# Five tiles of the last layer share their first and last score columns in 32x64 array tiles, under a new written-out order

## The chip, the cores and the metric

The kernel runs on one core of one Trainium2 chip. Its engines work side by side, each through its own list of instructions in order: TensorE (PE for matmuls, PEld for their weight loads), VectorE (DVE), ScalarE (ACT), GpSimd (POOL), and SyncE (SP), which here only issues DMAs. They wait for each other by semaphores. The metric is the time of one execution on the device in microseconds; less is better.

## The reference

A sequence of 2048 tokens of 512 features goes through four residual layers, x = x + f(layernorm(x)): linear attention (A), sliding-window attention (B), and both once more with the same weights. Each has 32 heads of 16 features.

```python
def _A_ref(x, wqkv, wo):
    phi = lambda t: jnp.where(t > 0, t + 1, jnp.exp(t)) + 1e-6
    pq, pk = phi(q), phi(k)
    kv = jnp.einsum("bhsd,bhse->bhde", pk, v)
    ...
    o = num / den
def _B_ref(x, wqkv, wo):
    scores = jnp.einsum("bhqd,bhkd->bhqk", q, k) * (Dh ** -0.5)
    mask = (idx[:, None] - idx[None, :] >= 0) & (idx[:, None] - idx[None, :] < W)   # W = 256
    p = _softmax(jnp.where(mask, scores, -1e9), axis=-1)
    o = jnp.einsum("bhqk,bhkd->bhqd", p, v)
```

In B a query sees itself and the 255 tokens before it. All values are bf16 in memory; matmuls accumulate in f32.

## The kernel before, in words

**Tiles.** The 2048 tokens are 16 tiles of 128, called j = 0 to 15 here. "Tiles ten to fourteen" of the change are j = 9 to 13. Activations stay in the core's memory from the first layer to the last.

**Scores of a sliding-window layer** (`b_scores`, `b_far`). Scores are computed with keys on the partitions. A tile's keys are two blocks (b = 0, 1) of 64; the 128 partitions of a block are 64 keys times two heads. The 32 heads are 16 pairs: four groups (f) of four (gq). A key of block b is seen by the queries from 64b of its tile on, over 64 + 255 places: a window of 320 columns. The first 64 are partly masked (a key does not see earlier queries), the last 64 as well (a query 256 later does not see it), the 192 between are whole. The window is computed in two pieces:

- `b_scores`, four times a tile (block b, groups f and f+1): 8 matmuls (L634) of 256 columns from column 0 of the window on. A matmul uses a 32-row by 128-column part of the array, and gq = 0 to 3 run in four such parts at once, into four banks of PSUM. Then two ACTIVATEs (L644) of 128x1024 take the exponential of two banks each into the buffer `P`, and a mask on DVE (L652) clears the forbidden part of the first 64 columns.
- `b_far`, once for each tile that has a tile two places later: 32 matmuls (L723) of the last 64 columns, for all f, b and gq, two ACTIVATEs (L732) of 128x1024, and two masks ("mf"), each on DVE (L704) or POOL (L703).

`P` has four slots in the last layer, used by j modulo 4. `b_values` (L753) multiplies the exponentials with the values; tile j's products read the slots of tiles j, j-1 and j-2, and of the far columns only those of tile j-2. Then come a reciprocal, a division, a transpose by DMA, the output projection and the residual.

**Beside it.** For later tiles the layer before's output (L400), the layer norm (statistics L361 and L362 on DVE, two small steps L363 and L364 on POOL, normalisation L365 on DVE, transposes by DMA) and the projections to queries, keys (L414) and values (L400) run ahead. Their results are evicted from PSUM by ACT or DVE, as the table says.

**What sets the order.** `Plan` adds all operations of the program to a list with what they read and write. `place` decodes `TABLE`, a long literal that holds three things: the order of all operations, the engine of each (where there is a choice), and the PSUM bank of each result. `synchronise` turns dependences into semaphore waits. `play` then emits each engine's operations in that order. So the order isn't computed at build time: it was made elsewhere, by a planner that replays the program, which the file does not contain. Each engine works strictly in the order written; an operation that waits holds all that stands behind it on its engine.

`PACK` says for which layer and tiles the window is computed in another way (`b_edge`); in the kernel before it is empty, so this function, though written, is not used.

Of the kernel before, what the change touches and what calls it, by code (L numbers as in the profile page):

```python
# [217 lines left out]
PACK = {}  # L218
# [5 lines left out]
def bass_view(x, free):  # L224

    return bass.AP(x.tensor, x.offset, [x.ap[0]] + free)


class Plan:
# [583 lines left out]
    def middle(self, ph):  # L813
# [67 lines left out]
    r"c-qx@1GF_svTkM|BlEXy+qP}nwr$(CZQHhO+vck}r|*5!Z@Oo?d-~nAZk@e%)sBq#BI5g^a@AfZlu{~$0;LryR$&yWuqvD~D!huXLaGNYf=Zwws)XvEi=-aA",  # L881
    r"L@KgMtdgiqN>mh;RNZ$?)pPgAJ#m@UXq8N5QOQ*^)k9@fR;5+VRSK0&jZy1WcGW_~QaRLEHCM$}#Z^@G%=J_oR7zD-#Zlu_OVvw_SFKbu_0&yJ2UTlTOZ8Tz",
    r")I1ekwNY(VP}N7(RvT4k^<AY?snjM_M0HW~Rb16hHBfa_Jk?O8R|`~86<haJ`PD?#PqkN*R8F-}HBxm|f0aiKP(M@#)j|DKG1Nd+Or=(v)nrvq9a0(97FA7k",
    r"RF_p(6;mBngH#%|NKH|LReg0tby8Q<QFT=fRa4b5wN-Uf*VH!kRFzSSRd=;rEm1?%b+uIOP&bs)&(sXHQ$1HRRcN(Ll~p12G?iB!S6ZJ?%N6JsDwmqBLg_gA",
    r"q*|$7s?a*Wo~3T8S1PT(rNZdAdWFiZPN~}}oerXQtJ5mI-lf87)baEk6;9t(XH*7Fy0I#tU#pC|pk_T=WzuKW9Cc3_{YJ&tqKByjx`2AChN~v3rY@-7sS)bF",
    r"s-;J&@cO+fq$B9kYLxn@N~nlBvo5TQ=t%m5imbEfggUEsDv{2ntxl}7>nJ*jE~=C2LaLZ{y0}iJE2|PZs!py;>Iy1{4z5b+e5$rCtb(bEx{l7N>*?XTk}j>A",
    r">&m){uA)|{7P_jgrbp=Nx`uA4SF5_Zl4_;bsHVD|ZmgT>J*u2)qZ{fby1s6$%d5Srfj+0!sz$o4KCddOeQKm$r$*`h>VlfBtE<s^j=rc4=`p&b`lPC=HF~U`",
    r"s}JjO`m>s+$Lj}bf_|tDsEK;MKBC*}NqT`^t1qdAdYWFOzo_YYonEXTsmZ#7e&c57y?TmXuV?Cxx|9B@rs`RGgWjh*>y7%d-mkmp<$9BTtXAmFdWn9bw&<05",
    r"ss5&}=w-UA4gy#8QGG)Pg=_kj?xu^uDt$~BhhT71AJ+%;6CFgK&`<SAy;YZhQ+k_zrh~%{9aJCG+x2t3Q<sEb`nrChcj?tSD!kOuAOr;0r644n)*<vOeMX0Z",
    r"(hwT%=;&}(hk<jthPtQE>xb@wzN@?IG7t}X=!^OkB!JVfN0)`_@LI=*a&QJ>K@GUAW5WoD2{mCP#DV*|HY9_D@J7GYF(5fS(C_p^Jqj-A6gmZ@)Q|LT9T&>O",  # L890
    r"d!0%@)~TQZeATISY8VY+Asmc>G>}G*g$NKHB0@zN2X$aPoP|U%0qQ~}hy;nD9-M=ox)!v6^N<88LsDo37hon_gjtXhT0&a*rY}Ji_^xL|1NfoSK_f^HKlN>B",
    r"2(96R&HxJP!ySkW8b0ZaFcI!Tc9;YJA9Wj;440uDTmgi}Ku|`1(QTouz6zNj3Y62Ibq>e^)gUJ{fvS)TGDB0C2hAWG<c2A*0H#8D&5#G?Lj|1|3^a#mS|A@R",
    r"ghh}QrolB>4A&t)SSSGPA-cW+OP~Wd=m;_NQdk9@Af{dhYhVt<(#v5kbcWT?ORs>Quo8Ofb+7^Y>4H!Q`s(!%2K(r+xE2b-6W9o^-7_cxn;;x+hNAEk!s7?1",
    r"h#%oORKhK=6?(xZsEoVe0Yt#wPz4`CM9ii8z<tQABjF?H3teCu&VZ_zM@Pon*bg2<6zm3Zu|MS1(=ng!3IiY>R>OgC2WQ|Qh>z9r4b;Fr&>h~wUbqK$u?O_m",
    r"@1Q2`gKaQCZ-*B!9bUp`*a5fTJ?w{McoV)r3OoR>;42)2*RTtc<4jD1QE{M7g5Mw-?u73!7@{L$VjKeLa3~ytx|k5tV+<Syvv4@X#MzhuQ(`8ZgGsR-X2w)l",
    r"A5&u%jD^kdFtos|SPPFpMy!o#uqCF&)>sD#+aO~ryocGaEgJj**)a~z#h=g!6JQQ(j5$%EU}roEO|T0tN5E!y47#Gm6__8pqs8OU4qv#H*dBZ0JiL!5paVX@",
    r"lh6YluEE&Y5er}t?1byEAojwC_|gT%ZnzeM;Rbw!y|EB(#6Gwln_^*n<u>7C%!Ng;FD}BO*bj5#V%&@ku^7(B;+O}Q;0`Q-3vd^{!G-u1^WjcxfP-{!9IS_6",
    r"UVMikaF~AULgF4AqE}-A+KZvEBo5W3a36-ogw!8P<4|0R1F#GZ!$h<SpWr|&i_7pSCZ;3!47cELJc?U!HzuJGcnp)$S8Ph#a6cxa@7Rn+Vsd(p%_#*9#&7rn",
    r"4`2&=iKFl%wxl0;5I^H~9F41J5FWx$xS9^*7(~iQt!OMVWun%UlG+f_8v1~#C=GqV%ybeB39Y5nbR5%?rJwj7(~+WA=;#EtrEH|>6awX-(>M;Z(-|C(K`0kZ",
    r"z_S>Xa??Z%M(1!6p2s|tlZsJRx`4syJ%ymxSb{##I?78OX+2%U;`EU&VIkT;ou~-qqmq<`I#YfsOyQ_E6`*!hkor(jYEPx8FLj{)^odH-0P07Vu?!8QD_E93",  # L900
    r"Q%KrKS1|((qVN=oBG5IgOxLj+g{JNlk#^H2ibOqVG=-%-G?pUMWK2(cX$nT6F;tGCQWg3_(WnAdrRWrfwox^jirc9?^`zmngTB&W>PjQ2It`&NG>%5lX8J}$",
    r"={p^u8dQmD(iS>I!zc!ArCt=1YSBSDLbYiW)u9`Blq%9q98b6K7)_v9bb%()aWZ_7CXw(A(tL?51IMN_beZbXSvpMh2zei!pmP+5_R~qKPv<EppQ0-ij89Vo",
    r"x=IZxIEQ4%*JvhPr%)V%XVG2yL9;0|N8}*<ljcw)&cbs^aaNv3k$E!Br$)4s7SI%GOxbuB-J>Qnl@`){ipmctE=A*M6pvc)LyFEf=n=K#=|p^s9@8U^Pt1?`",
    r"Cbi-xbeI=W7=FS}DK5w0BOH&P@@)#sQ8+#?rlTB=pYamP%i%dD=jRB#lw$ER%Evi5JKv$@l#8EHY+gYH_!zIG+<b;}@L4X(=lDDq=Qw<U^Kc?A#uvFHALr6s",
    r"kWX+SPROOWBbVUkT$np?8GgY<I01L&ww##TaS|@eNx40j<7E7j`*Jx<&i%Oyr{MC~fnRYyenTnwEmgn)+>^`mJL<~4xB_?M*W8<{@pDSWv$;FJpt;<GQ}Y}?",
    r"$$j`GRpeJRkSlQ;eoce8HCN_SJeaHV5I)UScqmWj8a$If@(ixYZ@3mO=TE$XXYop2%(b~HzvZP|hcog#Uc#C9GuP#1JdEFQJs!@hxIWM4%shfu^BNw>3wRW-",
    r"<u5#%)9^Z8$Z2^IkKs$4j>qzPZp!0$1E=T9{FSe82ENL5%|_nD+HB@)Jf62On5}%B(QM-zJb|}!Gv2`y`6kyhJGlYx;)dLur*I>l%8hw9Phv8AxC!6l_k5f8",
    r"@&~@d)A#`I<H>xG@A7^=#P|3<vw6S|`5R|8nap?2V}5WBlh@=jIZZZWOm6d&vzUBFnd~ON$!f$DFhPwq1x<b9OaoKcbTkc3CllT@GQmt|Gs^@wvrS`D$TTq#",
    r"OcyiQG&Ms^GZVx#H=#@m)76A9q0La!&9pILOi0t+v^70U5!24hF+I&x6VVJa?M+M5%M3RiOe+(~6g4AEKhxTbH2qCvQ_M^=1I#E>+=MmL&1f^wlrp`|7}LiL",
    r"G9}DdGsBcLea$!%&dfA>%y@Ijls0=!D4A<6n|)@3xne@gMl;V$FkxiAnP{$>O=f{PU<%1XbI?pOi%emuV^*6Ya>%?eQ_MB9##}eA%wx0G+%QkfOLNm~F;C4c",  # L910
    r"v)F7iVP%PlVxF0BveaxfQB8PxZVsDeCV~`|XlA`RVV0X>a>}eT5v91qG||mu6T`$ZCrt^tZ6e7EbH~Is+szwu*OZi%CXR_M`^{T(&#W?=O<Z%|yfbm+fhl9+",
    r"$`|v{lr=}pS98?FmmOxOIc6eDJUMQ@nfK<0DJ8E>6xn5dn$sq+*=?dq5_8rl`CvYpq((~ud1OABXp+n%lFuf(BsY~Mp_DT*#7Gsf^4-LgbEc}CH?c${iCi!s",
# [181 lines left out]
```

## Time and profile before

| | |
|---|---|
| runs shown | 416.35, 417.3, 420.33 us (median 417.3) |
| the profiled execution | 415.97 us |
| its span in the trace | 414.2 us, 17130 instructions |
| granted TensorE clock | 0.999 |
| busy, share of the span | PE 94%, DVE 84%, ACT 83%, PEld 62%, POOL 28% |
| ACTIVATEs for scores (L644, L732) | 256 and 56 |
| far masks on POOL, on DVE | 29, 27 |

The page counts busy time over the whole span. The layers differ in what limits them, so the stretches are what to look at: the second layer's scores run from about 60 us to 230 us, the last layer's from about 260 us to 406 us. A busy PE includes matmuls that are under way at the same time. "Wait" rows name the instruction that waited, what released it, the total, the number of times and the longest.

### The profile page before, as it was taken

The page shows a single profiled execution, that of the slowest core. Times are in us where ns is not written, and L with a number is a line of the kernel's source. Part 1 is how long each engine was busy: PE and PEld are TensorE (multiplying, and loading weights), DVE is VectorE, ACT ScalarE, POOL GpSimd, SP SyncE. Part 2 cuts the span into 40 slices and gives each one's busy share as a digit, 9 for nine tenths or more (in the row PEclk, how much of TensorE's full clock was granted, in tenths as well). Part 3 has the DMA queues.
Part 4 walks back from the last instruction along what each step waited for, and adds up shares of the span by engine and source line. Part 5 has one row for each costly group of instructions (what it writes and reads, how often), then busy time and mean ns, then how long its engine had stood idle before and what let it go on. Part 6 is the DMA issues. An engine that isn't in the chain of part 4 may idle for free.

```text
span 414.2 us, 17130 instructions
## 1 busy us (share of the span) xinstructions
PE 387.9 (94%) x7481; PEld 258.5 (62%) x7555; DVE 346.8 (84%) x803; ACT 345.8 (83%) x432; POOL 117.7 (28%) x211
## 2 busy tenths in 40 slices
PE   7999999999999999999999999999999989988886
PEld 3545676766575577565666777586757745556554
DVE  5997898989989988778978689989799687776575
ACT  2624449998999999999997245999999999999992
POOL 4784833111241243230112302220132215230111
PEclk9999999999999999999999999999999999999999
DMA  7545316632233624444213100353306623273361
GB/s 246 177 79 148 104 40 119 131 92 68 64 96 78 110 73 113 80 107 106 56 29 69 26 2 27 93 148 79 81 7 134 137 56 95 60 159 96 93 121 54
DMA packets 67555, 37.83 MB, mean 91 GB/s; under 512 B 48248, under 2 KB 62584, under 8 KB 67480
## 3 DMA queue, kind: packets, MB, share of 16 engines
q1 hardware_dynamic: 67040, 35.54, 36.7%
q8 instruction: 60, 0.98, 1.0%
q0 software_dynamic: 432, 1.18, 0.9%
q14 instruction: 15, 0.12, 0.1%
q10 hardware_dynamic: 8, 0.00, 0.0%
HBM read 6.29 MB, written 2.10 MB: 20 GB/s over the span
## 4 chain that ended last, share of the span: by engine, by line
PE 48%; ACT 35%; DVE 9%; DMA 5%; issue 2%; SPq 1%
ACT pb L644 22%; PE ps L400 17%; PE ps L414 13%; PE ps L753 7%; ACT pb L732 6%; ACT vp L644 5%; PE ps L634 5%; PE ps L475 2%; DMA XQ<-xn 2%; DVE stats L361 2%; DMA xres<-in_A_x_dram 2%; DVE xres L568 1%; DVE XQ L557 1%; PE ps L723 1%; ACT vp L732 1%
## 5 line engine op out<-in xcount | busy, mean ns | idle before, releaser
L644 ACT ACTIVATE pb<-ps 128x1024 bf16<-128x1024 f32 (+2 forms) x224 | 206.7, 1042 | 4.5 <-PE ps L634 3.7
L753 PEld LDWEIGHTS ps<-vB,pb 128*128 128x128 bf16 x2560 | 77.5, 96 | 11.7 <-issue 4.6
L753 PE MATMUL ps<-vB,pb 128*128 128x34 bf16 x2560 | 83.2, 177 | 1.1 <-ACT pb L644 0.6
L414 PE MATMUL ps<-xT,wBp 128*128 128x128 bf16 x1024 | 69.2, 219 | 1.2 <-DVE vp L586 0.5
L414 PEld LDWEIGHTS ps<-xT,wBp 128*128 128x128 bf16 x1024 | 59.2, 98 | 13.6 <-issue 4.4
L423 ACT ACTIVATE tE<-ps 128x512 bf16<-128x512 f32 x64 | 38.5, 612 | 34.3 <-PE ps L400 15.5
L363 POOL TENSOR_SCALAR ve<-mv 128x1 f32<-128x1 f32 x64 | 16.7, 261 | 172.6 <-DVE mv L362 170.5
L634 PE MATMUL ps<-XQ,kB 32*128 32x256 bf16 (+2 forms) x1024 | 49.6, 267 | 5.0 <-ACT vp L644 1.4
L732 ACT ACTIVATE pb<-ps 128x1024 bf16<-128x1024 f32 x50 | 49.6, 1066 | 0.4 <-PE ps L723 0.2
L568 DVE TENSOR_TENSOR xres<-ps,xres 128x512 bf16<-128x512 f32 x63 | 43.1, 685 | 7.6 <-PE ps L400 7.0
L400 PE MATMUL ps<-wA,XQ 128*128 128x512 bf16 x176 | 46.2, 379 | 2.7 <-issue 0.6
L652 DVE TENSOR_TENSOR pb<-pb,tri 128x512 bf16<-128x512 bf16 x112 | 44.7, 412 | 4.0 <-ACT pb L644 3.7
L703 POOL TENSOR_SCALAR_AFFINE_SELECT pb<-pb 128x1024 bf16<-128x1024 bf16 x26 | 29.8, 1148 | 62.9 <-DVE pb L652 32.6
L361 DVE BATCH_NORM_STATS2 stats<-xres 128x6 f32<-128x512 bf16 x64 | 43.6, 686 | 2.6 <-DMA xres<-in_A_x_dram 1.8
L364 POOL TENSOR_TENSOR rs<-ve,negh 128x1 f32<-128x1 f32 x64 | 37.8, 591 | 5.3
L634 PEld LDWEIGHTS ps<-XQ,kB 32*128 32x128 bf16 x1024 | 15.5, 92 | 33.6 <-ACT pb L644 9.2
L414 PE MATMUL ps<-XQ,wA 128*128 128x128 bf16 x512 | 34.7, 219 | 0.3 <-DVE o L766 0.3
L414 PEld LDWEIGHTS ps<-XQ,wA 128*128 128x128 bf16 x512 | 30.4, 98 | 5.7 <-DVE o L766 0.6
L400 PE MATMUL ps<-wBv,xT 128*128 128x512 bf16 x112 | 31.5, 380 | 2.2 <-issue 1.3
L400 PE MATMUL ps<-wBo,oT 128*128 128x512 bf16 x105 | 28.8, 380 | 4.2 <-issue 1.1
L400 PE MATMUL ps<-M,XQ 128*128 128x512 bf16 x112 | 30.7, 380 | 2.1 <-issue 1.0
L765 DVE RECIPROCAL rc<-ps 128x16 f32<-128x16 f32 x64 | 16.1, 252 | 19.3 <-PE ps L753 19.0
(110 smaller groups left out, 532.8 us busy)
## 6 DMA issues: line engine op xcount, KB each, us to landing
vB<-vS SPq DMA_DIRECT2D x64, 136.0 KB, 2.6
kB<-vp SPq DMA_DIRECT2D x64, 128.0 KB, 2.7
wA<-in_A_wqkv_dram SPq DMA_DIRECT2D x3, 512.0 KB, 4.6
out_dram<-xres POOLq DMA_DIRECT2D x9, 128.0 KB, 2.8
xres<-in_A_x_dram SPq DMA_DIRECT2D x2, 512.0 KB, 4.3
pb<-in_B_wqkv_dram SPq DMA_DIRECT2D x1, 1024.0 KB, 5.6
xres<-in_A_x_dram SPq DMA_DIRECT2D x3, 256.0 KB, 4.8
out_dram<-xres SPq DMA_DIRECT2D x6, 128.0 KB, 2.4
```

The lines of the kernel that those rows point to most:

```text
L361: self.on("DVE", "stats", lambda e: e.bn_stats(K.stats[:, t, :], K.xres[:, t, :]), key, dve(512), rd=[("xres", t)], wr=[("stats", t)])
L364: self.pow = self.on("POOL", "pow", lambda e: e.tensor_tensor(K.rs[:, t, :], K.ve[:, t, :], K.negh[:], ALU.pow), key + 0.03, (640, 690), r ...
L400: m = e.matmul(K.ps(ps), lhs(c), rhs(c), start=c == 0, stop=c == 3)
L414: m = e.matmul(K.ps(ps)[:, f * P:(f + 1) * P], w(c, f), xT(c), start=c == 0, stop=c == 3)
L423: self.on("ACT", "E", lambda e: e.activation(K.tE[:, s, :], K.ps(ps), ACT.Exp, bias=0.0), key, act(512), wr=[("tE", s)], ps=[ps])
L568: self.on("DVE", "res", lambda e: e.tensor_tensor(K.xres[:, t, :], K.ps(po), K.xres[:, t, :], ALU.add), key, dve(512), rd=[("xres", t)], w ...
L634: m = e.matmul(K.ps(ps[gq])[:, ns * i:ns * i + ns], K.kB[rows, j % 4, 2 * f + b, :, :], K.XQ[rows, f, q:q + ns], start=True, stop=True, ti ...
L644: return e.activation(out(2 * h, 2, ns), i, ACT.Exp, bias=0.0, scale=0.25)
L652: return e.tensor_tensor(x, x, K.tri[:, 0, sh:64].unsqueeze(1).unsqueeze(1).to_broadcast([P, 4, n, 64 - sh]), ALU.mult)
L703: return e.affine_select(out=x, in_=x, compare_op=ALU.is_ge, fill=0.0, base=-2, pattern=[[0, 16], [-2, 64]], channel_multiplier=1)
L732: return e.activation(far(h), i, ACT.Exp, bias=0.0, scale=0.25)
L753: m = e.matmul(K.ps(ps)[:, 34 * u:34 * u + 34], K.P((b // 2) % rp)[:, gq, f, o:o + P], K.vB[:, (b // 2) % 4, b % 2, r, :], start=i == 0, s ...
```

## The change

**The packing.** For the last layer, `PACK` now names j = 9 to 13. For these tiles `b_scores` computes the window's columns 32 to 287 instead of 0 to 255; it still has 8 matmuls of 256 columns and two ACTIVATEs of 128x1024, four times a tile. `b_edge` takes the place of `b_far` and computes what is left. Of the first 32 columns only the first 32 keys of a block are ever visible, and of the last 32 only the last 32 keys. So both halves share one bank row: the first 32 keys times the first 32 columns go to partitions 0 to 63, and the last 32 keys times the last 32 columns go to partitions 64 to 127. The old text of `b_edge` computed both for all keys and copied one half over ("gc"); the new one computes each with a 32-row by 64-column part of the array (eight at once), 64 matmuls of 32 columns. Two ACTIVATEs of 128x512 follow. They write the last 32 columns of the window; an operation on DVE ("ma", 64 partitions, 1024 elements each) copies partitions 0 to 63 from there to the first 32 columns and masks them. The diagonal mask ("md") then covers 32 columns where it covered 64. The two far masks stay as they are; they wait for the copy. The products of tile j wait for its copy too, since part of its first columns now comes from the edge.

**The table.** It is replaced as a whole. Read out, it holds 2553 operations where there were 2548 (the five copies). PE has 874 in both, DVE 802 in both, ACT 427 for 431, POOL 217 for 207, SP 233 for 234.

- ACT's order of the exponentials is nearly the old one; the far pairs of j = 9 to 13 are gone, and the edge pairs stand behind the first two to four exponentials of their own tile.
- Thirteen copies and evictions go from ACT to DVE, nine from DVE to ACT. Of those in the second layer's scores, three that ran on ACT between 147 and 157 us go to DVE.
- Of the far masks, seventeen go from DVE to POOL (eight of them in the second layer) and eight from POOL to DVE (three there).
- Four output DMAs go from POOL's queue to SP's, five the other way.
- On PE, DVE, POOL and SP many operations move by a place or two, some by more: the rearrangement of weights ("wp") and the setting of constants on POOL in the first 70 us, and the far masks.

```diff
-PACK = {}
+PACK = {3: (9, 10, 11, 12, 13, )}
...
             for f in range(4):
                 for b in range(2):
-                    q = P * j + 64 * b
                     for gq in range(4):
                         rows = slice(32 * gq, 32 * gq + 32)
-                        c = 128 * f + 64 * b
-                        m = e.matmul(K.ps(ps[gq])[:, c:c + 64], K.kB[rows, j % 4, 2 * f + b, :, :], bass_view(K.XQ[rows, f, q:q + 32], [[288, 2], [1, 32]]), start=True, stop=True, tile_position=(32 * gq, 0))
+                        c = 64 * f + 32 * b
+                        for u in range(2):
+                            q = P * j + 64 * b + 288 * u
+                            half = slice(64 * u, 64 * u + 64)
+                            m = e.matmul(K.PS[half, ps[gq].banks[0], c:c + 32], K.kB[rows, j % 4, 2 * f + b, 32 * u:32 * u + 32, :], K.XQ[rows, f, q:q + 32], start=True, stop=True, tile_position=(32 * gq, 64 * u))
...
-        self.pe("s", put, key, 1, 512, mode=(32, 128), occ=245, rd=[("kB", j % 4, 0), ("kB", j % 4, 1), ("XQ", j), ("XQ", j + 2)], ps=ps)
+        self.pe("s", put, key, 1, 256, mode=(32, 64), occ=540, rd=[("kB", j % 4, 0), ("kB", j % 4, 1), ("XQ", j), ("XQ", j + 2)], ps=ps)
...
-            side = lambda c, two=two: bass_view(K.PS[64:128, two[0].banks[0], c:c + 32], [[512 * (two[1].banks[0] - two[0].banks[0]), 2], [64, 8], [1, 32]])
-            self.on("DVE", "gc", lambda e, side=side: e.tensor_copy(side(0), side(32)), key, dve(512), ps=two)
...
-                return e.activation(edge(h), K.pair(two, [[128, 4], [64, 2], [1, 32]]), ACT.Exp, bias=0.0, scale=0.25)
+                return e.activation(edge(h), K.pair(two, [[64, 4], [32, 2], [1, 32]]), ACT.Exp, bias=0.0, scale=0.25)
...
 TABLE = (
-    r"c-qx@1GF_svTkM|BlEXy+qP}nwr$(CZQHhO+vck}r|*5!Z@Oo?d-~nAZk@e%)sBq#BI5g^a@AfZlu{~$0;LryR$&yWuqvD~D!huXLaGNYf=Zwws)XvEi=-aA",
...
+    r"c-qxi1Gsd{j;*AUO4V=Mwr$(CZQHhO+qP}nw$16?{qCFhX70W7&zn2nH?z;_uG*<&)yhhCo$eDtDHTeg0;LtJFp5-I6;2ryUd2}-)hic4B~UM1LiO4`agSXh",
...
 )
```

More of the change, by code (lines that the diff above doesn't have):

```diff
@@ L885 @@
[L885 to L900, printed above, removed]
@@ new lines @@
+    r"IHh)}mnsz8RHxM|6&h}-w4fmj+*V;>x0<cuK{&Xh2=c1C>a5DA&Zs$xp(ezK*UCTw5U2&k)f-h+<%j#~t!ko%smf}&N(b*$0Z0$`)O$5Tg@+6f0g9@OP!L9{",
+    r"Oz=TPgoIEC3d2Vg35q~uNCXxVgM(ly31o&*D!&S%vOrRZ0tHl7hzi*tIb?@YswfnLWKd8Qha6A>YC|zq5~{15P#SWpI#3y^Kq)Av>cJ{i2`WM%)f}oq3#bN#",
+    r"RduKVt5r*=3nf%5SfeVcrqCK1Lo?W;+CX_#ADX~9wN^ENwopkmguSW}w1e|%pIWCz!YJ6UE~p2pf*K98VGfLe8tS2%3!l_j_^jr^I5-3c)Oa`y^I;84fCX?-",
+    r"O@t$`7AC<$xTM;{G*|>*)H;|Bi(v#jQj?(r%z(X6O-+IIFbg_DCzuLf)lAq28=$o60vlmD?1z%-D6D|aumm>2N>~by)n>R1$6y(BgDr3cjzcl*3RmF-1i^3W",
@@ new lines @@
+    r"-jN@2SAy9J_MT+6_obrEVjJ4jwvugRv)Ts|+@`S)#o2X2HmzMRk0gTKAR%l-%l3(cv`;0H?P5dObT+iDX1dw*R@ufjgZ(L8Z4(>W7L+iyscmh;+BWu?gtKjJ",
+    r"4EtPS+3>cReId<lOq;{Duu*I-8^=bqIc;^5-A1#ICAzI);@Uj6rpad~*~zw+$!7D~DYl5MZHn2`cB(CEJJ@OVjGb;f*~Rv(one>Qmy+9dv?c608_$-sGi`jE",
+    r"-_EiLY$-d!R<;FfD?8Gjw@Yn7o5>cpqwEG-+7_~9Y;0TDZnT|kS-Z&&u<dO*JH`fa<!w7V$Od(@ZAKf+4YYl1RomUpv%y^z+t<#qA>4dB*Y>k(>;*g6_OKz{",
+    r"X1mrdus!WXd&#b|z3gQh%B`>=rMK;G^SYHbv|Ddi*&Q~YTWELM)%K2UY4f{X_Nm<{)$DUy-Cnmf>@$1U7I1s)ZoAhGvG?p~JJc3*`|LwI%ocLPZB2W_KDJ}+",
@@ L934 @@
+    r"frrKW#Lw)N)<YroausjM^D|lkA%U0t7VEFU-`NG89t{Dl{k34@zhRHA58Qi95ZNcW{x>8KJrw",
 )
```

79 lines of the change are left out of this document (43 added, 36 removed).

## The prediction

> **What bounds the kernel now.** I read the head of the page first, then the slices, then the busy time by stretches, and only then the chain of work that ended last.
>
> ```profile
> span 414.2 us, 17130 instructions
> ...
> PE 387.9 (94%) x7481; PEld 258.5 (62%) x7555; DVE 346.8 (84%) x803; ACT 345.8 (83%) x432; POOL 117.7 (28%) x211
> ...
> ACT  2624449998999999999997245999999999999992
> ```
>
> By the shares PE would be the bound and ACT third. The row of slices says otherwise for a part of the time: ACT is full in slices 8 to 22 and again from slice 25 to the last but one. The columns of the next view are the stretch, its length, and the busy time (with the count) of PE, PEld, DVE, ACT and POOL, then the granted clock and DMA.
>
> ```profile
> 100.00:150.00 50.00, 46.82 (x999) 29.77 (x1007) 46.53 (x110) 49.16 (x58) 11.91 (x22) 1.00 0.43 91
> ...
> 250.00:280.00 30.00, 29.41 (x518) 21.28 (x520) 27.81 (x64) 26.39 (x36) 7.87 (x16) 1.00 0.36 95
> ...
> 324.00:400.00 76.00, 67.28 (x1569) 43.95 (x1580) 55.43 (x125) 75.33 (x83) 16.81 (x23) 1.00 0.42 98
> ```
>
> From 324 to 400 us ACT works 75.33 of 76 us, while PE leaves 8.7 us and DVE 20.6 us free. PE can do better than that: from 250 to 280 it is busy 29.41 of 30 us, 98%. The chain agrees (start, length, what):
>
> ```profile
> 114.93 1.94 ACT pb L732 x2
> ...
> 161.13 9.20 ACT pb L644 x10
> ...
> 324.08 1.94 ACT vp L732 x2
> ...
> 399.74 0.71 ACT pb L644
> ```
>
> The last 76 us before the tail are, all but half a microsecond, one run of exponentials: nothing but ACT's own queue decides when they end, and tiles 9 to 13 of the last layer lie in its latter part. An exponential that becomes shorter there shortens the span, as long as PE keeps up. Between 115 and 170 us, in the first sliding-window layer, it is mostly the same.
>
> **The change, part by part.** *The exponentials.* Each of the five tiles loses its far pair (two ACTIVATEs of 128x1024, L732) and gets an edge pair of 128x512; its other eight stay 128x1024, only their window is shifted by 32 queries.
>
> ```profile
> L644 ACT ACTIVATE pb<-ps 128x1024 bf16<-128x1024 f32 x208 | 197.7, 1070 | 3.4 <-PE ps L634 2.8
> ...
> L732 ACT ACTIVATE pb<-ps 128x1024 bf16<-128x1024 f32 x50 | 49.6, 1066 | 0.4 <-PE ps L723 0.2
> ...
> L644 ACT ACTIVATE vp<-ps 128x512 bf16<-128x512 f32 x4 | 2.1, 594 | 0.1
> ```
>
> Neighbours on ACT overlap, so the price is the distance between starts, from rows of the timeline:
>
> ```profile
> 346.75 13.05 ACT L644 ACTIVATE pb<-ps 128x1024 bf16<-128x1024 f32 x14
> 379.85 14.38 ACT L644 ACTIVATE pb<-ps 128x1024 bf16<-128x1024 f32 x16
> 403.65 1.09 ACT L644 ACTIVATE vp<-ps 128x512 bf16<-128x512 f32 x2
> ```
>
> Taking one duration off each run, 13 + 15 distances take (13.05 - 1.07) + (14.38 - 1.07) = 25.3 us, 0.90 each. The half-sized pair: 1.09 - 0.59 = 0.50. So an edge exponential saves 0.40, ten save **4.0 us**. Bounds: 3.1 if the small ones don't overlap at all (0.90 - 0.59), 4.8 by the whole durations (1.07 - 0.59). The edge writes pieces of 32 columns where the far one writes 64; that pieces cost nothing is seen in 1066 against 1070 ns for pieces of 64 and of 256. I take 4.0, from the distances.
>
> *TensorE.* The far operation is 32 matmuls of 64 columns, four at a time; the edge is 64 of 32 columns, eight at a time. Two rows of the timeline (start, length from the first start to the last end) and one of the operation's own durations:
>
> ```profile
> 358.94 0.41 PE L723 MATMUL ps<-XQ,kB 32*128 32x64 bf16 x32
> 400.82 1.37 PE L753 MATMUL ps<-vB,pb 128*128 128x34 bf16 x48
> L723 PE MATMUL ps<-XQ,kB x896: 188/188/198, 86.6 to 397.5; 32*128 32x64 bf16 x180
> ```
>
> No 32x64 tile runs in this trace. The lower end is 0.41 us, as now (the columns streamed per tile are the same in all). At the far operation's spacing, (0.41 - 0.19)/31 = 7 ns, 64 of them take 0.64. At the spacing of whole-array matmuls, (1.37 - 0.18)/47 = 25 ns, they take 1.8. I take 0.64, by the row nearest in shape: 0.23 more for each tile, 1.2 us of PE in all. With 4 us less of ACT, PE would be busy (67.3 + 1.2) of 72 us, 95%, still under the 98% that it reaches elsewhere: hidden. If that cover goes, it is added whole.
>
> The Trainium skill, "TensorE: Matmul & The Clock Gate", section The mechanism, says that a weight load overlaps a running matmul only when their row groups differ. In the edge, every second load goes to the row group of the matmul just before it; in the far operation none does. By that rule the pairs serialise, and the sum would be that of the first rival.
>
> *VectorE.* These rows give one operation's shortest, median and longest duration in ns:
>
> ```profile
> L652 DVE TENSOR_TENSOR pb<-pb,tri x112: 361/418/427, 66.9 to 403.0; 128x512 bf16<-128x512 bf16 x112
> L704 DVE TENSOR_TENSOR pb<-pb,tri x24: 657/684/697, 89.8 to 400.4; 128x1024 bf16<-128x1024 bf16 x24
> ```
>
> The diagonal masks of these tiles shrink from 512 to 256 elements a partition. From 418 and 684 ns, 0.52 ns an element: 0.13 saved, times 20 masks, 2.7 us. The new copy-and-mask takes 1024 elements on half of the partitions, like L704: 0.68 times 5, 3.4 us. Net 0.7 us more, of 20.6 free. It adds a wait: the value products of a tile now wait for that tile's own edge and its copy; before, only the products two tiles later needed the far pair. The new table, read out, puts the edge exponentials behind the tile's first two to four, and the copy before or among its diagonal masks, ahead of the products; behind the copy in DVE's queue stand masks and divisions. I cost it at nothing, DVE's idle time being the cover. The edge also needs queries two tiles ahead sooner than the far pair did; the table has these queries' evictions well before it.
>
> *Delivery.* Two half-sized exponentials give PE 1.0 us to bring the next scores, where two whole ones gave 1.8. ACT waited 2.8 us in 208 instructions of L644 for scores; from nothing to one score operation of 0.4 each time (2.0 in all), I take 0.4.
>
> *The new order.* ACT's sequence is nearly the old one. Thirteen evictions leave ACT for DVE and nine come. Three leave in the run from 115 to 170 us, none comes there: 3 x 0.50 = 1.5 us. PE is busy 46.8 of 50 us beside it, so I take half, 0.8 (0 to 1.5). DVE, at 46.5 of 50, gets them, but the table also moves masks to POOL (8 in that layer, 3 back). All other reordering, most of it by a place or two, I take at nothing. The trace bounds it only widely: PE idles 414.2 - 387.9 = 26 us in all, and as much could be added; I allow 3 us either way.
>
> The sum: -4.0 + 0.4 - 0.8 = **-4.4 us**. The profiled execution took 415.97 us, 1.8 outside its span, so 411.6. The runs shown have a median of 417.3, 1.3 above it: 417.3 - 4.4 = **412.9**.
>
> **The rivals.** *First: the saving is eaten by PE.* With y more per edge, the stretch can't be shorter than (67.3 + 5y)/0.98. At y = 1.4, the 25 ns spacing, that is 75.8 us: all of the 4 us is gone, and 417 comes out (416.5 with half the evictions' gain). For it: PE is the nearest bound here, and the new tile shape has no row. Against it: the row of 7 ns for tiles side by side, and 8.7 us of room. To be slower by over 1% it would need y = 2.3, 42 ns a matmul.
>
> *Second, slower: POOL parks in front of a mask with a layer norm behind it.* POOL works in order; it makes the far masks and, between them, two small steps of each layer norm (L363, L364), on which the next tile's queries and keys hang. The table gives POOL ten more operations, nine of them masks. The rows: POOL's waits at masks; four of the timeline in order of time; the transposes (median us to landing); the masks' durations on POOL.
>
> ```profile
> POOL pb L703 <- DVE pb L652: 32.6, 9, 12.4
> 344.76 0.22 POOL L363 TENSOR_SCALAR ve<-mv 128x1 f32<-128x1 f32 x1 [1.15 <-DVE mv L362]
> 344.94 2.02 ACT L732 ACTIVATE pb<-ps 128x1024 bf16<-128x1024 f32 x2
> 349.75 0.41 DVE L365 TENSOR_SCALAR xn<-xres,mv,rs 128x512 bf16<-128x512 bf16 x1
> 359.90 1.05 PE L414 MATMUL ps<-xT,wBp 128*128 128x128 bf16 x16
> xT<-xn SPq DMA_TRANSPOSE x28, 2.7
> L703 POOL TENSOR_SCALAR_AFFINE_SELECT pb<-pb x26: 1146/1147/1167, 93.4 to 365.2; 128x1024 bf16<-128x1024 bf16 x26
> ```
>
> Already POOL stands at masks 32.6 us in nine waits, one of 12.4. A place where the new order does it: the small step at 344.76 (tile 13's norm) will stand behind three masks, the second of which needs the exponentials of 344.94 to 346.96. Two masks of 1.15 from there put it at 349.3, and its second step stands behind the first step of yet another norm; I estimate that the normalised tile comes 2 to 4 us after the 349.75 of now. Its product starts at 359.90, and the DVE step of 0.41 and a transpose of 2.7 lie between: 359.9 - 349.75 - 3.1 = 7 us to spare, so here it costs nothing. It decides where the wait outgrows such slack. One of 12.4 us costs 12.4 - 7 = 5.4; with that and no gain from the evictions it is 417.3 - 3.6 + 5.4 = 419.1, and with two of them 424.5. From 7.9 us of such excess on, it is slower by over 1%. Against it: POOL is busy only 16.8 of 76 us, and the table has the norms mostly ahead of masks whose data come late.
>
> The Trainium skill, "SBUF — State Buffer", section Who interferes with whom, adds that a DVE operation with two SBUF inputs and a POOL operation that reads SBUF block each other fully. This trace disagrees: 29 masks ran on POOL, and DVE's L704 never took more than 697 ns against a median of 684. By that rule eight or nine more masks would put some 10 us on DVE; by the row, nothing.
>
> *Third: the saving comes and the new order gives more*, up to its 3 us: 409.9.
>
> **How the numbers follow.** 1% of 417.3 is 4.2 us, about what a measurement of this kernel can tell from no change; my forecast lies just beyond it. Chances: forecast with the third case 0.55, the saving eaten or half eaten (413.5 to 418) 0.24, the norms held up or the new order worse in the PE-bound stretches 0.21. The forecast's own range, 409.9 to 414.5, has a part within 1%: about 0.48 for faster, 0.31 for within, 0.21 for slower. The range goes from 408.5 (all terms at their good ends: -4.8 - 1.5 - 3 gives 408.0) to 422, between the second rival's one wait and its two; I leave out some 0.07 below and 0.13 above.
>
> **What would show it.** Right: ten ACTIVATEs of 128x512 some 0.5 us apart behind tiles' first scores, ACT still full from 324 us to its last whole exponential, that run some 4 us shorter, PE at 95% in it; the edge's 64 matmuls within 0.7 us. Wrong by the first rival: edges of 1.5 us and more on PE, and ACT waiting for scores of L634 in the last 70 us. Wrong by the second: POOL's waits at masks longer than now, followed by DVE waiting for L364's result and ACT idle behind it. Wrong altogether if the stretch up to 280 us ends later by more than the tiles save: then the order decides, and the tile shape is innocent.

## The result and the profile after

| | before | after |
|---|---|---|
| median, same chip, alternating runs | 417.02 us (416.35 to 420.33) | 412.61 us (412.06 to 415.03) |
| ratio, 95% interval | | **0.9896** [0.986, 0.9932] |
| profiled execution, its span | 415.97, 414.2 us | 412.48, 410.8 us |

The changed kernel is 1.0% faster. A second comparison, over more runs (below), gives 0.9924 [0.99, 0.9949]. The head of the changed kernel's page:

```profile
span 410.8 us, 17457 instructions
...
PE 389.5 (95%) x7639; PEld 260.5 (63%) x7715; DVE 344.4 (84%) x803; ACT 341.9 (83%) x428; POOL 126.3 (31%) x221
```

ACT has 3.9 us less to do in the whole program (345.8 before), and the span is 3.4 us shorter. That looks like a clean exchange, and it isn't one. The stretch of the last layer's tiles, as in the prediction (busy time of PE, PEld, DVE, ACT, POOL, the granted clock, DMA):

```profile
324.00:400.00 76.00, 68.89 (x1765) 46.35 (x1773) 55.73 (x129) 73.77 (x87) 20.86 (x28) 1.00 0.40 104
```

In the last 76 us ACT now has 2.2 us free where it had 0.7: part of what the edges save is spent waiting. To see how much, I cut the span at four marks that exist in both kernels: the first score exponential of the second layer, the first of tile 9 in the last layer (ahead of it nothing is packed), the end of the last exponential, and the end. The first two, in rows of ACT's timeline of the changed kernel (start, length):

```profile
62.75 2.85 ACT L644 ACTIVATE pb<-ps 128x1024 bf16<-128x1024 f32 x3 [0.55 <-PE ps L634]
...
344.72 3.89 ACT L644 ACTIVATE pb<-ps 128x1024 bf16<-128x1024 f32 x4
```

Tile 9's mark before is at 346.75 (the prediction has the row), the first at 63.13:

```profile
63.13 3.77 ACT L644 ACTIVATE pb<-ps 128x1024 bf16<-128x1024 f32 x4
```

| stretch, us | before | after | difference |
|---|---|---|---|
| to the first score exponential | 63.13 | 62.75 | -0.4 |
| from there to tile 9 of the last layer | 283.62 | 281.97 | **-1.65** |
| tile 9 to the end of the last exponential | 59.53 | 58.47 | **-1.06** |
| from there to the end | 7.92 | 7.61 | -0.3 |

About half of the gain lies where no tile shape was changed: the second row. The first row is within what the traces vary by (this mark lies at 62.7 to 64.2 us in the traces of the unedited new order), the second isn't: in eight traces with the new order unedited up to tile 9 (the changed kernel's two and six of the experiments) it is 281.4 to 282.4. The packed tiles, for which I had forecast 3.6 us, gave about one. Within them, the busy time from tile 9's first exponential up to tile 15's last pair, first before, then after (one view, two kernels):

```profile
346.75:405.60 58.85, 52.16 (x1286) 35.16 (x1292) 41.72 (x97) 58.73 (x69) 12.10 (x18) 1.00 0.46 109
```
```profile
344.72:402.53 57.81, 53.11 (x1453) 37.24 (x1460) 40.57 (x100) 55.67 (x69) 17.09 (x23) 1.00 0.42 108
```

ACT idles 0.1 us in the first and 2.1 in the second. Counted by starts: the ten far exponentials took 9.13 us, the ten edges take 5.62, so 3.5 are saved; but the 44 whole exponentials in between (40 of the five tiles, four of tile 8), from start to start, went from 40.32 to 42.18, and tile 15's four of 128x512 from 1.97 to 2.67. The chain that ended last shows what stands between them now. Before, it was one unbroken run of ACT from 337.69 to 400.45 us; three of its pieces, then the chain after:

```profile
337.69 3.77 ACT vp L644 x4
...
346.97 12.84 ACT pb L644 x14
...
379.99 14.24 ACT pb L644 x16
```
```profile
335.67 2.86 ACT vp L644 x3
338.98 1.56 PE ps L400 x6
...
343.87 0.68 DVE vp L652 x2
344.59 1.37 PE ps L753 x48
...
351.50 0.87 PE ps L676 x64
352.39 1.08 ACT pb L685 x2
353.50 3.78 ACT pb L644 x4
357.32 1.37 PE ps L753 x48
360.64 5.61 ACT pb L644 x6
```

PE's products (L753) and projections (L400), and steps of DVE, take turns with the exponentials. The edges' own matmuls (L676) are among what comes late: PE waited for other engines ahead of them, 0.5 us for DVE's residual (L568) and 0.5 for an eviction of DVE (L389).

The pieces themselves came out as costed. An edge in the rows of the timeline:

```profile
351.50 0.68 PE L676 MATMUL ps<-XQ,kB 32*64 32x32 bf16 x64 [0.20 <-DVE xn L365]
...
352.39 1.08 ACT L685 ACTIVATE pb<-ps 128x512 bf16<-128x512 f32 x2
```

These 64 matmuls take 0.68 us (0.64 forecast; 0.68 to 0.77 over the five edges), the pair of exponentials starts 0.49 us apart (1.08 less one duration of 0.59).

### The profile page after: what moved, and what is told of

It reads as the page before. It is cut to its first block, busy times and chain, and to the rows that moved or that the text cites. A ratio compares the mean times of both kernels' runs of the same rounds, so it can differ in the third digit from the quotient of the medians.

```text
span 410.8 us, 17457 instructions
## 1 busy us (share of the span) xinstructions
PE 389.5 (95%) x7639; PEld 260.5 (63%) x7715; DVE 344.4 (84%) x803; ACT 341.9 (83%) x428; POOL 126.3 (31%) x221
## 4 chain that ended last, share of the span: by engine, by line
PE 60%; ACT 26%; DVE 10%; issue 2%; DMA 1%; POOL 0%; DVEq 0%; POOLq 0%; SPq 0%
PE ps L400 21%; ACT pb L644 16%; PE ps L414 14%; PE ps L753 8%; PE ps L634 5%; ACT pb L732 4%; PE ps L475 3%; ACT vp L644 3%; DVE XQ L557 2%; ACT tE L423 1%; PE ps L723 1%; DVE xres L568 1%; DMA kB<-vp 1%; PE ps L1007 1%; PE ps L451 1%
## 5 line engine op out<-in xcount | busy, mean ns | idle before, releaser
L753 PEld LDWEIGHTS ps<-vB,pb 128*128 128x128 bf16 x2560 | 77.7, 96 | 12.9 <-issue 3.7
L753 PE MATMUL ps<-vB,pb 128*128 128x34 bf16 x2560 | 83.8, 177 | 0.6 <-ACT pb L644 0.4
L414 PE MATMUL ps<-xT,wBp 128*128 128x128 bf16 x1024 | 69.1, 219 | 0.7 <-DVE stats L361 0.4
L414 PEld LDWEIGHTS ps<-xT,wBp 128*128 128x128 bf16 x1024 | 59.1, 98 | 12.2 <-issue 4.4
L703 POOL TENSOR_SCALAR_AFFINE_SELECT pb<-pb 128x1024 bf16<-128x1024 bf16 x33 | 37.8, 1145 | 82.6 <-ACT pb L732 30.1
L363 POOL TENSOR_SCALAR ve<-mv 128x1 f32<-128x1 f32 x64 | 15.6, 243 | 142.6 <-DVE mv L362 140.3
L568 DVE TENSOR_TENSOR xres<-ps,xres 128x512 bf16<-128x512 f32 x63 | 43.1, 684 | 8.8 <-PE ps L400 8.2
L400 PE MATMUL ps<-wA,XQ 128*128 128x512 bf16 x172 | 45.8, 379 | 2.1 <-issue 1.0
L652 DVE TENSOR_TENSOR pb<-pb,tri 128x512 bf16<-128x512 bf16 (+1 forms) x112 | 43.2, 398 | 2.2 <-ACT pb L644 2.1
L732 ACT ACTIVATE pb<-ps 128x1024 bf16<-128x1024 f32 x42 | 41.5, 1065 | 0.6 <-PE ps L723 0.4
L364 POOL TENSOR_TENSOR rs<-ve,negh 128x1 f32<-128x1 f32 x64 | 36.9, 577 | 5.3
L414 PE MATMUL ps<-XQ,wA 128*128 128x128 bf16 x512 | 35.5, 219 | 0.0
L414 PEld LDWEIGHTS ps<-XQ,wA 128*128 128x128 bf16 x512 | 30.7, 98 | 6.0 <-ACT pb L644 0.8
L400 PE MATMUL ps<-M,XQ 128*128 128x512 bf16 x113 | 30.9, 380 | 2.6 <-issue 1.0
L400 PE MATMUL ps<-wBv,xT 128*128 128x512 bf16 x111 | 31.1, 380 | 1.9 <-issue 1.1
L400 PE MATMUL ps<-wBo,oT 128*128 128x512 bf16 x107 | 29.7, 380 | 2.0 <-issue 0.6
L644 ACT ACTIVATE vp<-ps 128x1024 bf16<-128x1024 f32 (+2 forms) x32 | 26.6, 925 | 1.8 <-PE ps L634 1.8
```

What stands on the lines that cost most here:

```text
L364: self.pow = self.on("POOL", "pow", lambda e: e.tensor_tensor(K.rs[:, t, :], K.ve[:, t, :], K.negh[:], ALU.pow), key + 0.03, (640, 690), r ...
L400: m = e.matmul(K.ps(ps), lhs(c), rhs(c), start=c == 0, stop=c == 3)
L414: m = e.matmul(K.ps(ps)[:, f * P:(f + 1) * P], w(c, f), xT(c), start=c == 0, stop=c == 3)
L568: self.on("DVE", "res", lambda e: e.tensor_tensor(K.xres[:, t, :], K.ps(po), K.xres[:, t, :], ALU.add), key, dve(512), rd=[("xres", t)], w ...
L644: return e.activation(out(2 * h, 2, ns), i, ACT.Exp, bias=0.0, scale=0.25)
L652: return e.tensor_tensor(x, x, K.tri[:, 0, sh:64].unsqueeze(1).unsqueeze(1).to_broadcast([P, 4, n, 64 - sh]), ALU.mult)
```

## The experiments

Two theories. **ACT alone:** ACT's queue sets the end from tile 9 on, and what is taken from ACT comes off the time. **Coupled paces:** ACT, PE and DVE release one another so closely in the written-out order that what one engine saves waits for the next, and the order's own gain is a thing apart. A third, **PE alone**, is the prediction's first rival.

### The changed kernel again, the early order alone, the packed tiles alone, the far pairs halved

These four share the runs of the kernel before (median 416.87 us).

*after_again* is the changed kernel without an edit.

> The changed kernel once more, beside the others on one chip. All theories: 4.4 us below before (3.0 to 5.6).

Measured: 413.41 us, 0.9924 [0.99, 0.9949]. Its stretches are those of the first trace: 281.85 us from the first score exponential to tile 9, 58.51 from there to the last exponential.

*early_order* has the new order up to the scores of tile 9 of the last layer and the old one behind, and nothing packed. Its only edit of the kernel before is another table.

> The new order up to the scores of tile 9 of the last layer, then the old order, and no packing at all. Theory of two halves (from the traces: the changed kernel reaches tile 9 of the last layer 2.2 us sooner than the kernel before): 2.2 us below before (1.2 to 3.2). Rival, all of it is the packing: within 0.6 of before. Rival, all of it is the order: 4.4 below before.

Measured: 417.65 us, 1.0021 [1.0, 1.0041], no sign of the 2.2 us; by its time alone it would speak for "all of it is the packing". The new order brings it to tile 9 after 282.18 us, 1.4 less than before; but from there to the last exponential it takes 61.80 us, 2.3 more than before, some 1.5 of them at the seam. Three rows of the timeline at the seam, of ACT, DVE and POOL, and PE's only wait from 344 to 350 us:

```profile
348.38 3.77 ACT L644 ACTIVATE pb<-ps 128x1024 bf16<-128x1024 f32 x4 [1.27 <-PE ps L634]
...
344.78 1.35 DVE L652 TENSOR_TENSOR vp<-vp,tri 128x512 bf16<-128x512 bf16 x1
...
344.61 1.26 POOL L703 TENSOR_SCALAR_AFFINE_SELECT pb<-pb 128x1024 bf16<-128x1024 bf16 x1 [3.91 <-DVE vp L652]
```
```profile
PE ps L753 <- DVE vp L652: 1.4, 1, 1.4
```

A mask on DVE that takes 0.42 us elsewhere took 1.35, until just after POOL's mask had ended; the products waited 1.4 us for it, and ACT 1.27 for the scores queued on PE behind them. So the early order's gain stands in the traces alone; this run's time does not show it. This lengthening of DVE's mask comes up again below.

*late_packed* is the opposite: the old order up to tile 9, then the packed tiles in the new order, here against the kernel before (the text of `b_edge` and the table change with it).

```diff
-PACK = {}
+PACK = {3: (9, 10, 11, 12, 13, )}
...
```

> The old order up to the scores of tile 9 of the last layer, then the new order with the five packed tiles. Theory of two halves: 2.2 us below before (1.2 to 3.2). Rival, all packing: 4.4 below before, as the changed kernel. Rival, all order: within 0.6 of before.

Measured: 415.63 us, 0.9969 [0.9952, 0.9987], a gain of 1.2 us. From tile 9 to the last exponential it takes 59.08 us, against 59.53 before and 58.47 after, and 7.54 from there to the end, against 7.92 and 7.61. (The profiled execution took 418.81 us, with its excess ahead of tile 9, where 3.41 us ran at half clock; these later stretches are at full clock.) So the packed tiles, with their order and this seam, are worth about one microsecond, and that they are worth 3.6 falls.

*half_far* keeps the order of before and halves the columns of far exponentials, which leaves half of their values out: ACT's saving without the new order. It was meant for the ten of the last layer. But `K.rp` is read when the instructions are emitted, and by then it is 4 for both layers, so tiles 9 to 13 of the second layer are halved too: twenty exponentials, not ten.

```diff
         for h in range(2):
             def ex(e, h=h):
+                if K.rp == 4 and 9 <= j <= 13:
+                    o = bass_view(K.P(sl)[:, 2 * h, 0, 288:320], [[2816, 2], [704, 4], [384, 2], [1, 32]])
+                    return e.activation(o, pair(ps[2 * h:2 * h + 2], [[128, 4], [64, 2], [1, 32]]), ACT.Exp, bias=0.0, scale=0.25)
                 i = pair(ps[2 * h:2 * h + 2], [[128, 4], [64, 2], [1, 64]])
```

> The kernel before with its old order; only the ten far exponentials of tiles 9 to 13 of the last layer take half of their columns (the first 32 of each window's last 64 are left out, so the result is not the reference's). No packing, no copy, no new matmuls: ACT's saving by itself. If ACT alone sets the pace there, 3.5 to 4.2 us below before. If PE or DVE is close behind ACT, so that waits take up what ACT saves, 1 to 2.5 below before.

Measured: 416.16 us, 0.998 [0.9955, 1.0005], not clearly faster, with twice the intended cut. The shortened instructions (shortest, median and longest duration in ns, first and last start), and ACT's waits from 344 to 403 us (total, times, longest); in the kernel before, the same view of waits has no row at all:

```profile
L733 ACT ACTIVATE pb<-ps x18: 592/605/740, 175.2 to 399.5; 128x512 bf16<-128x512 f32 x18
L733 ACT ACTIVATE vp<-ps x2: 605/612/618, 378.8 to 379.2; 128x512 bf16<-128x512 f32 x2
...
ACT pb L644 <- PE ps L634: 2.0, 4, 0.8
ACT vp L644 <- PE ps L634: 0.9, 2, 0.5
ACT pb L733 <- PE ps L723: 0.2, 1, 0.2
```

In the last layer 4 us were taken from ACT, and 3.1 came back as waits for scores. From tile 9 to the last exponential the profiled execution (417.69 us, among the longest of its twelve) takes 60.24 us, even 0.7 more than before; besides its wait, an exponential that has waited loses its overlap with the one ahead (1.07 us from start to end, 0.90 from start to start). In the second layer the other 4 us bought nothing either: from its first score exponential to the last layer's it is 197.58 us, against 197.29 before. That is the plainest verdict on "ACT alone": in the kernel before, too, the scores arrived just in time, and a queue that is full is not yet the one that decides.

### The edges in the old order, the new order with far pairs; ACT and PE each cut

Four more, with their own runs of the kernel before (median 416.79 us). Against the changed kernel I set them by its two ratios: 412.5 to 413.6 us.

*old_order_edges* puts the edges into the old order by hand, near the places that the new order gives them, and takes the far pairs out (against the kernel before; the text of `b_edge` and the table change with it).

```diff
-PACK = {}
+PACK = {3: (9, 10, 11, 12, 13, )}
...
```

> The old order throughout, with the edges of tiles 9 to 13 dropped into it near the places that the new order gives them, and the far pairs taken out (no seam; a few PSUM banks are given anew). If shorter exponentials are enough by themselves, 3 us below before, as the changed kernel. If they pay only in an order made for them, 0 to 1.3 below before.

Measured: 424.4 us, 1.0178 [1.013, 1.0227], slower. *new_order_far* is the reverse: the new order with the far pairs back near their old places (against the changed kernel).

```diff
-PACK = {3: (9, 10, 11, 12, 13, )}
+PACK = {}
...
-                        for u in range(2):
-                            q = P * j + 64 * b + 288 * u
...
```

> The new order throughout, with the edges taken out and the far pairs put back near their old places (79 of 1013 PSUM results get another bank). If the new order is the gain, 2 to 3 us below before. If it pays only together with the edges, between 1 below and 1 above before. If the changed kernel is the plain sum of the two, this and the old order with edges add up to 3.2 below before.

Measured: 429.2 us, 1.0293 [1.0258, 1.0327]. What PE's weight loads waited for from 344 to 410 us, in this kernel, most of all:

```profile
PEld ps L634 <- ACT pb L732: 6.1, 3, 2.2
```

Scores wait for PSUM banks that the far pairs still hold. Neither run prices the tile shape by itself: in both some results also had to be given other banks (79 of 1013 in new_order_far), so they show only that order, banks and shape are one unit, and that these two exchanges by hand end 8 and 12 us above the kernel before. Both missed every expectation.

*less_act* cuts the edge exponentials of the changed kernel to a quarter. The expectation put that at 2.5 us less on ACT; the pages say 3.0 (338.9 us busy, 341.9 in the changed kernel).

```diff
-                return e.activation(edge(h), K.pair(two, [[64, 4], [32, 2], [1, 32]]), ACT.Exp, bias=0.0, scale=0.25)
+                o = bass_view(K.P(sl)[:, 2 * h, 0, 288:320], [[2816, 2], [384, 2], [1, 32]])
+                return e.activation(o, K.pair(two, [[32, 2], [1, 32]]), ACT.Exp, bias=0.0, scale=0.25)
```

> The changed kernel with edge exponentials of 128x128 in place of 128x512 (three quarters of their columns left out, so the result is not the reference's): some 0.25 us less for each, 2.5 us less of ACT where the packed tiles are. If ACT sets the pace there, 5.0 to 5.7 below before (2 to 2.5 below the changed kernel). If PE's order and its waits do, within 0.8 of the changed kernel, 2.4 to 4.0 below before.

Measured: 412.34 us, 0.9893 [0.9858, 0.9927], 0.1 to 1.3 us under the changed kernel, between the two expectations. From tile 9 to the last exponential 57.79 us, 0.7 less. ACT's waits from 344 to 403 us, first of the changed kernel, then of this one:

```profile
ACT vp L644 <- PE ps L634: 1.2, 3, 0.6
ACT pb L685 <- PE ps L676: 0.2, 1, 0.2
ACT vp L685 <- PE ps L676: 0.2, 1, 0.2
ACT pb L644 <- PE ps L634: 0.2, 1, 0.2
```
```profile
ACT pb L644 <- PE ps L634: 2.4, 5, 0.9
ACT vp L644 <- PE ps L634: 1.2, 3, 0.6
ACT pb L686 <- PE ps L676: 0.2, 1, 0.2
```

The waits rise from 1.8 to 3.8 us: 2.0 of the 3.0 saved.

*less_pe* replaces the edge's 64 matmuls by 4 of 256 columns, about 2.1 us less on PE (0.29 us each edge for 0.68 to 0.77).

```diff
-            for f in range(4):
-                for b in range(2):
-                    for gq in range(4):
...
+            for gq in range(4):
+                rows = slice(32 * gq, 32 * gq + 32)
+                m = e.matmul(K.ps(ps[gq])[:, 0:256], K.kB[rows, j % 4, 0, :, :], K.XQ[rows, 0, P * j:P * j + 256], start=True, stop=True, tile_position=(32 * gq, 0))
```

> The changed kernel with each edge's 64 matmuls of 32x64 tiles replaced by four of 32x128 with 256 columns, on wrong operands (it fills the same PSUM cells with other scores, so the result is not the reference's): some 0.45 us less of PE for each of five tiles, 2.2 us in all. If PE sets the pace there, 4.7 to 5.4 below before. If ACT does, within 0.8 of the changed kernel.

Measured: 413.41 us, 0.9929 [0.9901, 0.9958]: the changed kernel's time. PE's edges do not set the time either, and the first rival, by which they would eat the saving, falls. In its trace tile 9 to the last exponential is 0.8 us shorter, but the rest takes 8.62 us where it took 7.61: a transpose by DMA of 3.94 us stands there in the chain.

### Both cuts at once, VectorE cut, and the loads raised

The last four have a median before of 416.33 us; by the two ratios the changed kernel stands at 412.0 to 413.2.

*less_act_pe* has both edits.

> The changed kernel with both cuts of the last job at once: the edge exponentials on 128x128 (2.5 us less of ScalarE) and the edge's 64 matmuls replaced by 4 (2.2 us less of TensorE). This leaves out part of the computation, the scores of the edge columns and most of their exponentials. Each cut alone gave 1.3 us and 0 us below the changed kernel. ScalarE alone: -1.3, as with the first cut. Coupled paces: what each cut alone leaves waiting for the other comes free, -2 to -3.5. TensorE alone: 0 to -0.5.

Measured: 412.38 us, 0.9917 [0.9889, 0.9945]: again the changed kernel's time. The trace tells why it shows so little. Tile 9 to the last exponential takes 56.89 us, 1.6 less than in the changed kernel and just the sum of the two cuts alone (0.7 and 0.8). But 8.36 us follow it, 0.75 more than there. Its chain at the end:

```profile
397.96 1.30 PE ps L748 x48
400.19 3.64 DMA oT<-o
405.14 1.01 PE ps L795 x6
```

A transpose by DMA of 3.64 us stands where the changed kernel's chain has matmuls. That is some 5 us off two engines, 1.6 off the exponentials, and under 1 off the time. The -2 to -3.5 expected of coupled paces did not come: the tail behind the exponentials takes about half of their gain back in this trace. By the time alone, "TensorE alone" with its 0 to -0.5 fits; less_pe, where the same cut of PE took nothing off the time, and the 1.6 us off the exponentials speak against it.

*less_dve* cuts the copy-and-mask ("ma") to a sixteenth, about 2.5 us less on DVE (0.18 us a copy for 0.68), which leaves out most of the first columns.

```diff
-            x = lambda c: bass_view(K.P(sl)[0:64, 0, 0, c:c + 32], [[704, 16], [384, 2], [1, 32]])
-            return e.tensor_tensor(x(0), x(288), K.tri[0:64, 0, 0:32].unsqueeze(1).unsqueeze(1).to_broadcast([64, 16, 2, 32]), ALU.mult)
+            x = lambda c: bass_view(K.P(sl)[0:64, 0, 0, c:c + 32], [[704, 1], [384, 2], [1, 32]])
+            return e.tensor_tensor(x(0), x(288), K.tri[0:64, 0, 0:32].unsqueeze(1).unsqueeze(1).to_broadcast([64, 1, 2, 32]), ALU.mult)
```

> The changed kernel with the copy-and-mask of the edge columns cut to one sixteenth of its elements, which leaves out most of the masked first columns: some 0.6 us less of VectorE for each of the five tiles, 3 us in all, and the copy's result, for which the products wait, that much sooner. If VectorE's new work is hidden, as the prediction had it: within 0.5 us of the changed kernel. If the copy and the wait behind it hold up the products: -1 to -3.

Measured: 412.36 us, 0.9921 [0.989, 0.9951]. The copy and the new wait behind it are hidden, as forecast.

*more_act* issues an extra ACTIVATE of 128x512 ahead of each edge exponential.

```diff
+                e.activation(bass_view(K.P(sl)[:, 2 * h, 0, 320:384], [[2816, 2], [704, 4], [1, 64]]), K.pair(two, [[64, 4], [1, 64]]), ACT.Exp, bias=0.0, scale=0.25)
                 return e.activation(edge(h), K.pair(two, [[64, 4], [32, 2], [1, 32]]), ACT.Exp, bias=0.0, scale=0.25)
```

> The changed kernel with one ACTIVATE of 128x512 more ahead of each of the ten edge exponentials: it takes the exponential of the same scores into columns of the buffer that nothing reads. Ten times 0.50 us is 5.0 us more on ScalarE, and nothing on the other engines. Against the changed kernel of the same job: if ScalarE's queue alone sets the pace from tile 9 to 14, +5.0 us; if ScalarE is one of several coupled paces, as the run with shorter edges suggests (1.3 us for 2.5), between +2 and +4; if TensorE sets it, under +1.

Measured: 418.52 us, 1.0049 [1.0027, 1.0071], 5.3 to 6.5 us over the changed kernel: more than the 5.0 that were put in. *more_pe* issues the edge's matmuls twice.

```diff
-            for f in range(4):
+            for f in [0, 1, 2, 3, 0, 1, 2, 3]:
```

> The changed kernel with each edge's 64 matmuls issued twice, the second time over the first: 320 more matmuls, 0.6 us more of TensorE for each of the five tiles, 3 us in all. ScalarE alone as the pace: under +0.5 us where the scores are ready early, at most +1.5 where they come just in time. TensorE as the pace: +3. Coupled paces: +1 to +2.

Measured: 424.15 us, 1.0184 [1.0165, 1.0203], 11 to 12 us over the changed kernel for some 3 us of matmuls. The first is near the 5.0 of ACT alone, the second beyond every expectation. Two things show in the traces. The first is PE's waits of more_pe from 344 to 400 us; "issue" is time in which the engine waited for nothing that the profile shows:

```profile
PE ps L414 <- issue: 1.7, 1, 1.7
PE ps L676 <- issue: 1.2, 1, 1.2
PE ps L753 <- issue: 0.8, 1, 0.8
PE ps L634 <- issue: 0.7, 1, 0.7
```

Four stops of 4.4 us together, the longest just behind an edge of 128 matmuls in 1.21 us (five matmuls of L414 lie between), the one of 1.2 within an edge, after 100 of its matmuls; the changed kernel's PE has none over 0.24 us. That the instructions could not be brought as fast as the short matmuls used them up is my reading. The trace fits it: each stop ends 1.2 to 1.8 us after a transfer of 16 KB of the kind "instruction" (queue q8) has ended. It is not shown, since such transfers are as frequent in the changed kernel, where nothing stops. The second is the granted clock (the column behind POOL's), in more_pe and in more_act:

```profile
351.75:355.16 3.41, 1.91 (x82) 0.93 (x71) 0.90 (x4) 1.37 (x4) 0.01 (x1) 1.00 0.68 191
355.16:358.57 3.41, 3.41 (x16) 0.94 (x15) 1.25 (x2) 3.20 (x4) 0.00 (x0) 0.50 0.03 8
```
```profile
370.36:373.77 3.41, 1.96 (x88) 1.59 (x88) 1.69 (x5) 3.35 (x7) 0.00 (x0) 1.00 0.49 143
373.77:377.18 3.41, 3.41 (x23) 0.89 (x16) 0.84 (x2) 2.48 (x3) 0.00 (x0) 0.50 0.30 77
```

After a stretch of 3.41 us in which PE is busy only 1.9 or 2.0 us, the next 3.41 us run at half clock. A hold-up can thus be paid twice: once as idle time, once as a slow stretch that loses up to 1.7 us. Each of the two traces has two such slow stretches, and in more_pe the parts add up: 3 us of matmuls, 4.4 of stops and up to 3.4 of slow clock, of the 11 to 12. So these runs are lopsided: taking 2 to 5 us from one or two engines gives at most 1.3, while adding 3 to 5 costs all of it and more. So neither of the two raised loads gives a price of ACT or of PE alone, and they don't tell the theories apart; the cuts do.

## Why the prediction was right, and where it was not

The time, 412.9, lay 0.3 us from the median, and the difference of 4.4 us is that of the first comparison (3.5 by the second, and by the two profiled executions). But the sum behind it came out by luck: two errors of opposite sign. By the traces, which differ by 3.4 us, it had 2.5 us too much for the tiles and 1.5 too little for all the rest.

- **"Nothing but ACT's own queue decides"** fell. It is the step that made 3.6 us out of the tiles, and half_far refutes it for the kernel before (8 us off ACT in two layers, under 2 off the time), less_act for the kernel after. The full row of ACT and the chain's unbroken run were read rightly as far as they go; what they can't show is that the scores were only just in time.
- **The edge's distance, 0.50 for 0.90**, held: 0.49 in the pair's row, 3.5 us saved with the edges' own waits (4.0 forecast).
- **Delivery, +0.4 (0 to 2.0)** was the mis-sized term: the 44 whole exponentials stretched by 1.9 us, tile 15's four by another 0.7, together 2.6, over the upper bound. I had looked at ACT's idle time in the kernel before, which is small just because ACT's length gave PE its time.
- **The edge on PE, 0.64 us**, measured 0.68 to 0.77. By the spacing of whole-array matmuls it would have been 1.8. The rule of the Trainium skill, "TensorE: Matmul & The Clock Gate", section The mechanism, by which I had the pairs serialise, isn't borne out: (0.68 - 0.19) / 63 is 8 ns a matmul (9 in the slowest edge), hardly more than the far operation's 7. That PE would be at 95% in the stretch came out as 91% (68.89 of 76).
- **DVE, 0.7 us net, hidden**: held in size (283 ns the smaller mask, 677 the copy, medians) and in effect (less_dve), but for the one copy of 1.32 us below.
- **The evictions of the second layer, -0.8** did not show. From tile 4's last pair of exponentials (113 us) to the last layer's first exponential the stretch is 147.47 us before and 147.41 after. What was saved at ACT there was not waited for, as half_far found in the same stretch.
- **The rest of the order, 0 (3 either way)** brought -1.65 us, in two places: 1.0 between the first scores and 113 us (49.82 to 48.86), 0.8 from the last layer's first exponential to its tile 4's (41.42 to 40.59). Both repeat in the traces of other kernels: the first is 49.8 in half_far and old_order_edges, which have the old order there, and 48.7 to 48.9 in early_order and every trace of the changed kernel, edited or not; the second is 41.3 to 41.4 and 40.5 to 40.6. Here the third rival came true in part. Which of the many moves gave them was not tried.
- **The second rival, POOL parked ahead of a norm**, did not come, though POOL did park, longer than before. From 324 to 400 us:

```profile
POOL pb L703 <- ACT pb L732: 15.7, 1, 15.7
```

No hold-up behind it shows in the chain.
- **The row against the SBUF rule** was misread. I held that the trace disagrees with the Trainium skill, "SBUF — State Buffer", section Who interferes with whom, because masks on POOL and long masks on DVE were there without any slow one. They were there, but hardly ever at the same time: in the trace before, two such masks on DVE start within a POOL mask, 0.11 and 0.07 us before its end. In the changed kernel three start well within one. Two of them, DVE's timeline and then POOL's:

```profile
345.08 0.95 DVE L652 TENSOR_TENSOR pb<-pb,tri 128x512 bf16<-128x512 bf16 x1
...
388.66 1.32 DVE L691 TENSOR_TENSOR pb<-pb,tri 64x1024 bf16<-64x1024 bf16 x1
```
```profile
344.62 1.14 POOL L703 TENSOR_SCALAR_AFFINE_SELECT pb<-pb 128x1024 bf16<-128x1024 bf16 x1 [4.25 <-DVE vp L652]
...
388.30 1.15 POOL L703 TENSOR_SCALAR_AFFINE_SELECT pb<-pb 128x1024 bf16<-128x1024 bf16 x1
```

The first (0.42 elsewhere) ends 0.27 us after POOL's mask, the second (0.68 elsewhere) 0.53 after it: each still needs its own time less 0.15 us once POOL is done, as if nearly all of its work had waited. So the trace agrees with the page: the one that starts first has the port, and the other waits. The 10 us that I derived assumed that every mask collides; here they were 0.5 and 0.6 us longer, and the third, at 139.61 us, 0.3.

## What to carry to other kernels

An engine that is full and fills the chain sets the end only if its inputs are early; where nothing shows how early they are, make the engine's work shorter in one run and see what comes back as waits, before counting a saving in full. In an order written out in full, with banks given by hand, shape and order are one thing: price a change with its order, and expect part of the gain, or all of it, from places that the change does not name. And a trace without a slowdown says nothing of a conflict until it is seen that the two operations overlap in it at all.

## What the runs showed of the hardware that I had not expected

- **The clock follows idle time within the kernel.** In more_pe, more_act, new_order_far and late_packed stretches of 3.41 us at half clock came right after stretches of the same length in which PE was busy 0.5 to 0.6 of the time (once, in more_act, 0.70). The Trainium skill, "TensorE: Matmul & The Clock Gate", section What's actually happening, has a free-running window of 3413 ns after which an idle array is gated to half; the length agrees. Where the bound lies is not settled: early_order and half_far each have one stretch of 0.58, and new_order_far one of 0.42, with the full clock behind it. The changed kernel's lowest is about 0.66 (2.27 of 3.41 us), and its clock stayed whole up to 409 us.
- **PE stopped behind long runs of short matmuls.** 128 in 1.21 us were followed by a stop of 1.73 us, where 64 in 0.68 us were followed by none over 0.24. The cause is not shown.
- **A DVE operation with two inputs in SBUF that meets a running POOL mask ends only after it**, however short it is: less_dve's copy of 64x64, 0.18 us elsewhere, took 0.82 and ended 0.03 us after POOL's mask (timeline of DVE in less_dve). The masks of 0.42 ended 0.27 after theirs, the copy of 0.68 0.53 after: in each case its own time less 0.15 us.

```profile
388.13 0.82 DVE L691 TENSOR_TENSOR pb<-pb,tri 64x64 bf16<-64x64 bf16 x1
```
